# A fused attention and two mixture-of-experts layers: no score block computed twice, and the split of the turned p moved three slots ahead of its products

## The chip, the cores and the metric

One core of a Trainium2 chip runs the whole program. The metric is the device time of one execution in microseconds. TensorE (PE) does the matrix products, VectorE (DVE), ScalarE (ACT) and GpSimd (POOL) the elementwise work, SyncE (SP) issues nearly all transfers between memory and the chip's buffers.

## The reference

```
# attention without softmax: B = 8 batches, S = 3072 rows, D = 256, z has 64 columns
scores = z @ z.T / S
x = u * (max(scores, 0)**2 @ v)
# first expert layer on all 24576 rows of x: F = 1024
h = x @ w_in
solu = h * softmax(h)
ln = (solu - mean) / sqrt(var + 1e-6) * g_ln
x = ln @ w_out
# second layer: each row goes to the one of 8 experts with the largest gate
out[row] = gate * (max(x[row] @ w1[e], 0) @ w2[e])
```

## The kernel before, in words

The rows of all batches are cut into 48 chunks of 512 rows, six to a batch (below, chunk j is the chunk number j = 0 to 5 of its batch). A chunk is worked on in 24 slots, one for each block of 128 key rows. For a slot, scores come from two matmuls (`pe_scores`), ACT takes relu and square (`r`, then `a`), ACT writes the high part `ah` and DVE the low part `al` of each value (32-bit values are multiplied as sums of two parts), and PE adds six products of 512 columns to the chunk's output `o` (`pe_av`). The order of the work is written out by hand: a loop runs over slots n, and in slot n the scores of slot n + 4 (`LA` = 4) are issued, then the events that stand in a table for this slot, then `o` of slot n, then ACT's `ah` of slot n + 3 and DVE's `al` of slot n + 2. Each engine carries out its own instructions in this order.

Scores are symmetric. A block of chunk q against keys of chunk k > q is the turned block of chunk k against keys of chunk q. So the chunk that comes first stores its blocks turned (`put`: DVE transposes `a` into a buffer `sym`, one slot later SP sends it to `kept` in memory), and the later one reads them (`get`, four issues of 64 KB, 7 slots ahead of `o`: `LA` + `GA`) instead of computing. For blocks at least four chunks apart (`turn_late`) the transposing is done after the reading. One pair is left out by `again`: chunk 5 computes its four blocks against chunk 4 a second time, and chunk 4 does not store them. `order` spreads stored and computed blocks evenly over a chunk's 24 slots.

When a chunk's `o` is done, it is multiplied by u (`gate_x`, which writes `ut`) and split (`split_x`, which writes `xt`), and the first expert layer of that chunk runs as events in the 24 slots of the next one, in four blocks of 128 rows, t = 0 to 3, 6 slots apart. With w the first slot of a block: h on PE at w and w + 1, its maximum on DVE at w + 1 (line 491), the exponential on ACT and its product with h on DVE at w + 2, the 32 x 32 turning of p on DVE at w + 3 (`blk_turn`, line 512), the variance on ACT at w + 4. To finish turning, p goes through memory: `blk_put` at w + 3 writes `pb` to `moved` (line 521), `blk_get` at w + 5 reads it back as `pT` (line 527). `blk_split` makes the high half `pth` on ACT and the low half `ptl` on DVE (lines 104 and 105, in the helper `split`), in two halves at w + 9 and w + 10, and `blk_y` multiplies them with w_out at w + 10 and w + 11 (12 products each, lines 108 to 110 in the helper `mm3`). The steps that scale, route and scatter the rows follow from the slots after. The last chunk uses wider steps. After the 48th chunk the second expert layer runs over sorted rows until the end.

Of the kernel before, what the change touches and what calls it, by code (L numbers as in the profile page):

```python
# [33 lines left out]
def attention_moe_kernel(ctx, tc, u, v, z, w_in, w_out, g_ln, w_gate, w1, w2, out):  # L34
# [9 lines left out]
    NCB = S // CH  # L44
    NKB = S // P
# [4 lines left out]
    ZB = 5  # L50
# [3 lines left out]
    ZL = 8  # L54
    XA, XT0, XE = 2, 21, 23
    SA, SB, SC, SD, SH = 11, 14, 16, 19, 1
    TW, TM, X2 = 8, 2, 23
# [12 lines left out]
    SNAP = NCHUNK - 4  # L70
# [42 lines left out]
    with tc.manual_schedule():  # L113
# [4 lines left out]
                        base=-1, pattern=[[1, P]], channel_multiplier=-1)  # L118
# [13 lines left out]
    with ExitStack() as st:  # L132
# [20 lines left out]
        def at(slot, fn, *args):  # L153
            events[slot].append((fn, args))
# [3 lines left out]
        t = vp.tile([P, 2, 4, D], F32R, tag="vw", name="raw64").bitcast(I32).rearrange("p a r d -> p (a r d)")  # L158
        raw64 = [t[:, i * 2 * CH:(i + 1) * 2 * CH].rearrange("p (f two) -> p f two", two=2) for i in range(2)]
        t = mp.tile([P, F], F32, tag="pT", name="cu64").bitcast(I32)  # L160
# [159 lines left out]

        def again(q, k):
            return q == NCB - 2 and k == NCB - 1

        def turn_late(q, k):
            return q + 4 <= k

# [1 line left out]
        for par in range(min(2, B)):  # L331
            for hi in range(NCB):
                for lo in range(hi):
                    if again(lo, hi):
                        continue
                    kept[par, hi, lo] = nc.dram_tensor(f"kept_{par}_{hi}_{lo}", (4, P, CH), F32, kind="Internal").ap()
        t = [xrow.tile([P, KD * CH], F32, tag="x", name="sym") for _ in range(2)]
        t = [x[:, i * CH:(i + 1) * CH] for x in t for i in range(2)]
# [2 lines left out]

        def order(j):

            old = [kb for kb in range(4 * j) if not again(kb // 4, j)]
            new = [kb for kb in range(NKB) if kb not in old]
            return [kb for _, kb in sorted([((i + 0.5) / len(old), kb) for i, kb in enumerate(old)] +
                                           [((i + 0.5) / len(new), kb) for i, kb in enumerate(new)])]

# [7 lines left out]

        def is_kept(n):
            _, q, k, _ = block(n)
            return k < q and not again(k, q)

        def is_put(n):
            _, q, k, _ = block(n)
            return k > q and not again(q, k)

        n_put, n_get = [0], [0]
        put_t = {}
# [454 lines left out]
        for i in range(NU):  # L821
            w = HALF if i < N_CUT else units[i]
# [71 lines left out]
        for c in range(NCHUNK):  # L894
            b, j = divmod(c, NCB)
            s0 = c * NKB
            sb = b * NCB * NKB
            if b == 0:
                base = 4 * j - Z0
                zload = base - 5 + (j > 0)  # L900
                vload = 4 * j - V0
                at(base, turn_z, c)
            else:

                late = j >= NCB - 2
                base = sb + 3 + 4 * (j - NCB + 2) if late else sb - (NCB - 1 - j) * NKB + ZB
                zload = base - (4 if late else ZL)
                vload = sb - NKB + VL + VS * j
                at(base - 2, turn_z, c)
            at(zload, load_z, c)  # L910
            at(base, prep_z, c)
            if c > 0:
                at(s0 - LA - 5, swap_z, c)
            vstep = 3 if b else 2
            for h in range(2):
                at(vload + vstep * h, load_v, c, h)
                at(vload + vstep * (h + 1), prep_v, c, h)
            for x in range(4):
                at(s0 + 2 + x, load_u, c, x)
            at(s0 + 14, turn_u, c)  # L920

            last = c == NCHUNK - 1
            more = 2 if last else 1
            s1 = s0 + NKB
            for t in range(4):
                w = s1 + 2 + (TW if last else 6) * t
                at(w, blk_h, c, t, 0)
                at(w + 1, blk_h, c, t, 1)
                at(w + 1, blk_max, c, t)
                at(w + 2, blk_exp, c, t)  # L930
                at(w + 2, blk_mul, c, t)
                at(w + 3, blk_turn, c, t)
                at(w + 4, blk_var, c, t)
                at(w + 3, blk_put, c, t)
                at(w + 5, blk_get, c, t)
                y = w + 10 + TM * (t == 3 and last)
                at(y - 1, blk_split, c, t, 0)
                at(y, blk_split, c, t, 1)
                at(y, blk_y, c, t, 0)
                at(y + 1, blk_y, c, t, 1)  # L940
            e = y + 3
            for i in range(3):
                at(e + more * i, blk_scale, c, i)
            for i in range(2):
                at(e + more * (3 + i), blk_scale, c, 3)
            at(e + more * 5, blk_logits, c)
            for i in range(10):
                at(e + more * (6 + i + 2 * (i > 5)), blk_route, c, i)
            for t in range(4):
                at(e + more * (6 + 2 * t), blk_rows, c, t)  # L950
                at(e + more * (18 + 2 * t), blk_scatter, c, t)
# [7 lines left out]
        early = [(0, n_early, FULL)], False  # L959
        late = [(n_early, n_late, FULL), (n_early + n_late, n_half, HALF)], True  # L960
        for i in range(NE + 4):
            at((SNAP + 1) * NKB + 21 + 2 * i, table_step, 0, *early)
            at(after + 2 * i, table_step, 1, *late)
            at(after + 2 * i + 1, table_step, 1)
            if i < NE:
                at(after + 2 * i + 2, pad_tail, i)
# [113 lines left out]
```

## Time and profile before

| | |
|---|---|
| median of 3 runs | 4622.75 us (4619.26 to 4626.38) |
| profiled execution | 4625.15 us, its span 4623.4 us |
| busy: PE, DVE, ACT, POOL | 94%, 69%, 61%, 25% of the span |
| mean granted clock of TensorE | 0.986 of full speed |
| attention with the first expert layer | 0 to about 3393 us |
| second expert layer | from there to the end |

A busy share is an average over stages; the waits say what an engine stood idle for, and a stretch of one chunk shows what an average hides. SP has no busy share in the page: its timeline of issues shows it.

### The profile page before, as it was taken

Reading aid. Unit: us, or ns where it says so; the run is one execution under the profiler, and the core shown is the slowest. Engines: PE = TensorE matmul, PEld = TensorE weight load, DVE = VectorE, ACT = ScalarE, POOL = GpSimd, SP = SyncE. Lnnn points to the kernel's source line nnn. Section 1 sums busy time; section 2 is a strip of 40 time slices with the busy share of each in tenths; the row PEclk is TensorE's granted clock in tenths of the full one; section 3 lists DMA queues with packets and bytes.
Section 4 is the critical chain, followed back from the end, with each engine's and each line's share of the span. In section 5 each row is a group of like instructions: output and inputs, shape, how many; then the busy total and the mean of one; then the engine's idle time right before and its main releaser. Section 6 shows DMA issues by size and latency. Waiting matters only on the chain.

```text
span 4623.4 us, 74108 instructions
## 1 busy us (share of the span) xinstructions
PE 4344.6 (94%) x23458; PEld 3707.2 (80%) x23458; DVE 3195.8 (69%) x5636; ACT 2811.0 (61%) x5184; POOL 1174.6 (25%) x2346
## 2 busy tenths in 40 slices
PE   7999999999999999999999999899899999999998
PEld 5777777777777777777777777777789999999998
DVE  7677667767677766777676667767676665556676
ACT  6666665666576666656765766676454444444565
POOL 3123222322322222223222222222222211111111
PEclk8999999999999999999999999999999999999999
DMA  5687688778867886887688678767875655555575
GB/s 143 151 163 149 152 165 155 161 157 162 152 156 158 160 156 152 163 155 164 150 164 148 157 163 157 151 158 157 148 161 141 161 139 145 143 139 137 152 217 160
DMA packets 2529035, 719.21 MB, mean 156 GB/s; under 512 B 2326653, under 2 KB 2417021, under 8 KB 2528640
## 3 DMA queue, kind: packets, MB, share of 16 engines
q1 hardware_dynamic: 2509536, 663.33, 68.3%
q0 software_dynamic: 19104, 51.15, 3.3%
q8 instruction: 183, 3.00, 0.3%
q14 instruction: 212, 1.74, 0.1%
HBM read 442.46 MB, written 273.49 MB: 155 GB/s over the span
## 4 chain that ended last, share of the span: by engine, by line
PE 41%; SPq 18%; DVE 16%; DMA 15%; issue 5%; ACT 3%; POOL 0%; DVEq 0%; ACTq 0%; POOLq 0%
SPq L527 6%; SPq L391 6%; DMA sym<-kept 4%; DMA kept<-sym 4%; PE y L110 3%; PE y L108 3%; PE y L109 3%; PE g L109 3%; PE g L108 3%; PE g L110 3%; PE o L108 3%; PE o L109 3%; PE o L110 3%; PE yp L110 3%; DVE ptl L105 3%
## 5 line engine op out<-in xcount | busy, mean ns | idle before, releaser
L108 PE MATMUL o<-ah,vw 128*128 128x512 f32 x2304 | 923.3, 401 | 10.2 <-DVE ut L452 9.2
L109 PE MATMUL o<-al,vw 128*128 128x512 f32 x2304 | 915.7, 397 | 12.0 <-DVE al L428 12.0
L110 PE MATMUL o<-ah,vw 128*128 128x512 f32 x2304 | 907.4, 394 | 0.0
L413 ACT ACTIVATE r<-s 128x512 f32<-128x512 f32 x704 | 412.9, 587 | 446.4 <-PE s L408 446.3
L110 PE MATMUL yp<-gw,ptl 128*128 128x264 f32 x1536 | 471.9, 307 | 200.7 <-DVE ptl L105 199.8
L491 DVE TENSOR_REDUCE nm<-h 128x1 f32<-128x1024 f32 x192 | 234.9, 1223 | 555.7 <-PE h L479 553.4
L423 ACT ACTIVATE ah<-a 128x512 fp32r<-128x512 f32 x800 | 505.3, 632 | 134.3 <-PE o L110 39.4
L428 DVE TENSOR_TENSOR al<-a,ah 128x512 fp32r<-128x512 f32 x800 | 552.4, 693 | 10.3 <-ACT ah L423 8.8
L108 PEld LDWEIGHTS o<-ah,vw 128*128 128x128 f32 x2304 | 440.4, 191 | 103.4 <-DVE ut L452 19.2
L110 PEld LDWEIGHTS o<-ah,vw 128*128 128x128 f32 x2304 | 439.5, 191 | 97.3
L109 PEld LDWEIGHTS o<-al,vw 128*128 128x128 f32 x2304 | 440.3, 191 | 95.9 <-DVE al L428 17.6
L110 PEld LDWEIGHTS yp<-gw,ptl 128*128 128x128 f32 x1536 | 297.6, 194 | 250.9 <-DVE ptl L105 249.2
L108 PE MATMUL yp<-gw,pth 128*128 128x264 f32 x1536 | 450.6, 293 | 16.3 <-ACT pth L104 14.0
L418 ACT ACTIVATE a<-r 128x512 f32<-128x512 f32 x704 | 437.8, 622 | 26.6 <-DVE ps L632 12.9
L109 PE MATMUL yp<-gw,pth 128*128 128x264 f32 x1536 | 444.8, 290 | 0.0
L847 ACT ACTIVATE zw_x<-g 128x512 fp32r<-128x512 f32 (+1 forms) x350 | 182.6, 522 | 396.0 <-PE g L110 391.9
L848 DVE SCALAR_TENSOR_TENSOR zw_x<-g,zw_x 128x512 fp32r<-128x512 f32 (+1 forms) x350 | 208.4, 595 | 266.1 <-ACT zw_x L847 260.9
L496 ACT ACTIVATE p<-h,nm 128x1024 f32<-128x1024 f32 x192 | 214.3, 1116 | 267.5 <-DVE nm L491 267.4
L108 PEld LDWEIGHTS yp<-gw,pth 128*128 128x128 f32 x1536 | 295.9, 193 | 56.2 <-ACT pth L104 38.8
L377 DVE STREAM_TRANSPOSE sym<-a 128x512 f32<-128x512 f32 x352 | 248.6, 706 | 116.6 <-DMA kept<-sym 115.7
L508 ACT ACTIVATE p<-p,nmp 128x1024 f32<-128x1024 f32 x192 | 220.3, 1147 | 142.3 <-DVE pb L512 142.2
L644 POOL DMA_INDIRECT sorted_rows<-y,pi x192 | 200.9, 1046 | 409.8 <-DMA sorted_rows<-y,pi 346.7
(274 smaller groups left out, 10862.1 us busy)
## 6 DMA issues: line engine op xcount, KB each, us to landing
vw_x<-in_moe_w SPq DMA_DIRECT2D x124, 1024.0 KB, 5.4
sym<-kept SPq DMA_DIRECT2D x1792, 64.0 KB, 2.9
moved<-pb SPq DMA_DIRECT2D x768, 128.0 KB, 2.2
pT<-moved SPq DMA_DIRECT2D x768, 128.0 KB, 3.7
kept<-sym SPq DMA_DIRECT2D x352, 256.0 KB, 2.9
vr<-in_v SPq DMA_DIRECT2D x96, 256.0 KB, 2.9
ur<-in_u SPq DMA_DIRECT2D x384, 64.0 KB, 2.6
kept<-a SPq DMA_DIRECT2D x96, 256.0 KB, 3.4
```

The costliest lines, as they stand in the source:

```text
L108: T.matmul(out=out, lhsT=lh, rhs=rh, start=start, stop=False, **kw)
L109: T.matmul(out=out, lhsT=lh, rhs=rl, start=False, stop=False, **kw)
L110: T.matmul(out=out, lhsT=ll, rhs=rh, start=False, stop=stop, **kw)
L377: V.transpose(out=w, in_=a_t[n])
L391: nc.sync.dma_start(out=w[x * 32:(x + 1) * 32].rearrange("i (b j) -> i b j", j=32), in_=src[r, x])
L413: A.activation(out=r, in_=s_t.pop(n), func=AF.Relu)
L418: A.activation(out=a, in_=r_t.pop(n), func=AF.Square)
L423: A.activation(out=h, in_=a_t[n], func=AF.Copy)
L428: V.tensor_tensor(out=l, in0=a_t[n], in1=ah_t[n].bitcast(F32), op=ALU.subtract)
L491: V.tensor_reduce(out=s["nm"][:, t:t + 1], in_=h, axis=AX.X, op=ALU.max, negate=True)
L508: A.activation(out=p, in_=p, func=AF.Square, bias=s["nmp"][:, t:t + 1], accum_out=s["q"][:, t:t + 1])
L527: nc.sync.dma_start(out=w[y * 32:(y + 1) * 32].rearrange("j (a i) -> j a i", i=32), in_=src[y])
```

## The change

Four things change. The exception `again` goes: chunk 4 stores its four blocks against chunk 5, and chunk 5 reads them back, so that 20 of its 24 blocks are read and 4 computed. For all chunks but the last the put of p is moved from w + 3 to w + 4, the get from w + 5 to w + 8, the split from w + 9 and w + 10 to w + 12 and w + 13, the products from w + 10 and w + 11 to w + 15 and w + 16; scaling, routing and scattering follow the products and so move by 5 slots. The loads of z of the last two chunks of the next batch, which came late because the old rows were needed longer, now come by the rule of the others. A step that makes the table of experts moves by 5 slots.

```diff
--- before.py
+++ after.py
@@ -320,10 +320,6 @@
 
 
 
-
-        def again(q, k):
-            return q == NCB - 2 and k == NCB - 1
-
         def turn_late(q, k):
             return q + 4 <= k
 
@@ -331,8 +327,6 @@
         for par in range(min(2, B)):
             for hi in range(NCB):
                 for lo in range(hi):
-                    if again(lo, hi):
-                        continue
                     kept[par, hi, lo] = nc.dram_tensor(f"kept_{par}_{hi}_{lo}", (4, P, CH), F32, kind="Internal").ap()
         t = [xrow.tile([P, KD * CH], F32, tag="x", name="sym") for _ in range(2)]
         t = [x[:, i * CH:(i + 1) * CH] for x in t for i in range(2)]
@@ -341,8 +335,8 @@
 
         def order(j):
 
-            old = [kb for kb in range(4 * j) if not again(kb // 4, j)]
-            new = [kb for kb in range(NKB) if kb not in old]
+            old = list(range(4 * j))
+            new = list(range(4 * j, NKB))
             return [kb for _, kb in sorted([((i + 0.5) / len(old), kb) for i, kb in enumerate(old)] +
                                            [((i + 0.5) / len(new), kb) for i, kb in enumerate(new)])]
 
@@ -356,11 +350,11 @@
 
         def is_kept(n):
             _, q, k, _ = block(n)
-            return k < q and not again(k, q)
+            return k < q
 
         def is_put(n):
             _, q, k, _ = block(n)
-            return k > q and not again(q, k)
+            return k > q
 
         n_put, n_get = [0], [0]
         put_t = {}
@@ -901,10 +895,8 @@
                 vload = 4 * j - V0
                 at(base, turn_z, c)
             else:
-
-                late = j >= NCB - 2
-                base = sb + 3 + 4 * (j - NCB + 2) if late else sb - (NCB - 1 - j) * NKB + ZB
-                zload = base - (4 if late else ZL)
+                base = sb - (NCB - 1 - j) * NKB + ZB
+                zload = base - ZL
                 vload = sb - NKB + VL + VS * j
                 at(base - 2, turn_z, c)
             at(zload, load_z, c)
@@ -931,11 +923,13 @@
                 at(w + 2, blk_mul, c, t)
                 at(w + 3, blk_turn, c, t)
                 at(w + 4, blk_var, c, t)
-                at(w + 3, blk_put, c, t)
-                at(w + 5, blk_get, c, t)
-                y = w + 10 + TM * (t == 3 and last)
-                at(y - 1, blk_split, c, t, 0)
-                at(y, blk_split, c, t, 1)
+
+                out_, back, cut_, y = (3, 5, 9 + TM * (t == 3), 10 + TM * (t == 3)) if last else (4, 8, 12, 15)
+                at(w + out_, blk_put, c, t)
+                at(w + back, blk_get, c, t)
+                cut_, y = w + cut_, w + y
+                at(cut_, blk_split, c, t, 0)
+                at(cut_ + 1, blk_split, c, t, 1)
                 at(y, blk_y, c, t, 0)
                 at(y + 1, blk_y, c, t, 1)
             e = y + 3
@@ -959,7 +953,7 @@
         early = [(0, n_early, FULL)], False
         late = [(n_early, n_late, FULL), (n_early + n_late, n_half, HALF)], True
         for i in range(NE + 4):
-            at((SNAP + 1) * NKB + 21 + 2 * i, table_step, 0, *early)
+            at((SNAP + 1) * NKB + 26 + 2 * i, table_step, 0, *early)
             at(after + 2 * i, table_step, 1, *late)
             at(after + 2 * i + 1, table_step, 1)
             if i < NE:
```

On DVE, the last block of chunk 2 shows where the split stands before the sum of its products. In the kernel before, L105 writes `ptl` from `pT`, L428 is `al`, L512 turns p, and L550 takes the finished product `yp`:

```order
L105 TENSOR_TENSOR ptl_3296<-pT,pth_3295 128x512
L512 STREAM_TRANSPOSE pb<-p 128x1024
L285 TENSOR_TENSOR zw<-zt,zw 64x512
L428 TENSOR_TENSOR al<-a,ah 128x512
L105 TENSOR_TENSOR ptl_3328<-pT,pth_3327 128x512
L428 TENSOR_TENSOR al<-sym,ah 128x512
L550 SCALAR_TENSOR_TENSOR y<-gw_sum,nmp,yp 128x264
```

In the changed kernel (line numbers lower by 6: L422 is `al`, L485 the maximum, L495 and L497 the product with h, L506 the turning, L371 a `put`, L544 takes `yp`) the same block reads:

```order
L105 TENSOR_TENSOR ptl_3350<-pT,pth_3349 128x512
L422 TENSOR_TENSOR al<-a,ah 128x512
L105 TENSOR_TENSOR ptl_3378<-pT,pth_3377 128x512
L485 TENSOR_REDUCE nm<-h 128x1
L422 TENSOR_TENSOR al<-sym_151,ah 128x512
L495 SCALAR_TENSOR_TENSOR p,spm<-h,p 128x1024
L497 TENSOR_SCALAR nmp<-spm 128x1
L422 TENSOR_TENSOR al<-sym_152,ah 128x512
L506 STREAM_TRANSPOSE pb<-p 128x1024
L422 TENSOR_TENSOR al<-a,ah 128x512
L371 STREAM_TRANSPOSE sym<-a 128x512
L544 SCALAR_TENSOR_TENSOR y<-gw_sum,nmp,yp 128x264
```

Between the second half's split and the taking of `yp` stand now three `al` and the maximum, product and turning of another block, where one `al` stood before.

On SP, the middle of chunk 4 of the second batch. Before (L391 a get from `kept`, L521 a put of p, L527 a get of p, `x4` four issues):

```order
L521 DMA moved_1<-pb_8159 32x1024 x4
L391 DMA sym1_152<-kept_1_4_3 32x16x32 x4
L527 DMA pT_8241<-moved_1 32x32x32 x4
L391 DMA sym2_153<-kept_1_4_3 32x16x32 x4
L391 DMA sym3_154<-kept_1_4_3 32x16x32 x4
L391 DMA sym_150<-kept_1_4_3 32x16x32 x4
L521 DMA moved_2<-pb_8345 32x1024 x4
L391 DMA sym_150<-kept_1_5_0 32x16x32 x4
L527 DMA pT_8418<-moved_2 32x32x32 x4
L391 DMA sym0_151<-kept_1_5_0 32x16x32 x4
```

And after (L385 a get, L515 a put of p, L521 now the get of p, L377 a store of chunk 4's blocks, L268 a load of z):

```order
L515 DMA moved_1<-pb_8121 32x1024 x4
L377 DMA kept_1_5_4<-sym_149 128x512
L385 DMA sym0_151<-kept_1_4_3 32x16x32 x4
L385 DMA sym1_152<-kept_1_4_3 32x16x32 x4
L377 DMA kept_1_5_4<-sym_149 128x512
L521 DMA pT_8263<-moved_1 32x32x32 x4
L385 DMA sym2_153<-kept_1_4_3 32x16x32 x4
L385 DMA sym3_154<-kept_1_5_0 32x16x32 x4
L515 DMA moved_2<-pb_8309 32x1024 x4
L377 DMA kept_1_5_4<-sym_149 128x512
L385 DMA sym_150<-kept_1_5_0 32x16x32 x8
L268 DMA zd_8429<-in_z 32x16x32 x4
```

Stores and a load of z stand in a stretch that had none, and the get of p (`pT`) follows its put (`moved`) at a greater distance.

## Rows read from the trace of the kernel before

**Rows 1.** Profile page, part 1: busy time, share of the span, instructions.

```profile
PE 4344.6 (94%) x23458; PEld 3707.2 (80%) x23458; DVE 3195.8 (69%) x5636; ACT 2811.0 (61%) x5184; POOL 1174.6 (25%) x2346
```

**Rows 2.** PE's waits, whole span: who waited for whom, us, times, longest.

```profile
PE yp L110 <- DVE ptl L105: 199.8, 217, 4.7
PE yp L108 <- ACT pth L104: 14.0, 19, 1.5
PE o L109 <- DVE al L428: 12.0, 10, 2.8
PE o L108 <- DVE ut L452: 9.2, 34, 1.0
```

**Rows 3.** Waits of all engines, whole span, same columns.

```profile
PEld yp L110 <- DVE ptl L105: 249.2, 228, 4.9
ACT ah L423 <- DMA sym<-kept: 40.8, 41, 1.9
```

**Rows 4.** Timeline, one block: start, length in us, engine, line, operation, idle before.

```profile
1501.91 0.28 PE L108 MATMUL yp<-gw,pth 128*128 128x264 f32 x1
1502.03 0.28 PE L109 MATMUL yp<-gw,pth 128*128 128x264 f32 x1
1502.20 0.69 DVE L105 TENSOR_TENSOR ptl<-pT,pth 128x512 fp32r<-128x512 f32 x1
1502.94 0.39 PE L110 MATMUL yp<-gw,ptl 128*128 128x264 f32 x1 [0.63 <-DVE ptl L105]
```

**Rows 5.** Stretches of chunks 0, 1 and 4 of the third batch.

```profile
core 0: us, PE busy (x) PEld busy (x) DVE busy (x) ACT busy (x) POOL busy (x), PEclk, DMA share, GB/s
861.90:940.50 78.60, 70.97 (x337) 59.20 (x336) 56.52 (x96) 55.52 (x100) 22.54 (x48) 0.95 0.70 168
940.50:1011.50 71.00, 67.27 (x330) 55.94 (x329) 49.59 (x87) 51.43 (x93) 17.10 (x42) 0.99 0.70 156
...
1147.50:1213.90 66.40, 62.07 (x307) 50.80 (x306) 45.22 (x78) 38.27 (x69) 18.52 (x42) 1.00 0.86 147
```

**Rows 6.** Timeline of SP, chunk 4 of that batch, first and last rows.

```profile
1147.59 1.82 SPq L521 DMA_DIRECT2D moved<-pb  x4
...
1203.26 6.63 SPq L391 DMA_DIRECT2D sym<-kept  x12
1212.80 2.23 SPq L521 DMA_DIRECT2D moved<-pb  x4
```

**Rows 7.** PE's waits behind 3393 us.

```profile
PE yp L110 <- DVE ptl L105: 1.8, 4, 1.2
```

**Rows 8.** SP's own waits, whole span, the longest in total.

```profile
SPq L521 <- DVE pb L512: 420.5, 135, 7.6
```

**Rows 9.** Timeline of PE, a score pair's first and the matmul behind it.

```profile
1508.43 0.39 PE L407 MATMUL s<-zw 128*128 128x512 f32 x1
1508.88 0.40 PE L475 MATMUL h<-w_in,xt 128*128 128x512 f32 x1
```

**Rows 10.** Costliest groups by line: count, busy us, mean ns of one.

```profile
L413 ACT ACTIVATE r<-s 128x512 f32<-128x512 f32 x704 | 412.9, 587 | 446.4 <-PE s L408 446.3
L377 DVE STREAM_TRANSPOSE sym<-a 128x512 f32<-128x512 f32 x352 | 248.6, 706 | 116.6 <-DMA kept<-sym 115.7
```

**Rows 11.** Timeline, one store of a kept block.

```profile
1499.91 0.43 SPq L383 DMA_DIRECT2D kept<-sym  x1
```

**Rows 12.** Transfers in chunk 4: packets, main queue, one kind of issue.

```profile
DMA packets 56524, 9.75 MB, mean 148 GB/s; under 512 B 55852, under 2 KB 55852, under 8 KB 56518
q1 hardware_dynamic: 56326, 9.13, 83.7%
sym<-kept SPq DMA_DIRECT2D x64, 64.0 KB, 3.1
```

**Rows 13.** PE's waits in chunks 0 to 2, then 3 to 5.

```profile
PE yp L110 <- DVE ptl L105: 13.9, 13, 4.1
...
PE yp L110 <- DVE ptl L105: 10.7, 14, 1.3
```

## The prediction

> **What bounds the kernel now.** I first read how busy each engine is: TensorE (PE) works 94% of the span, VectorE (DVE) 69%, ScalarE (ACT) 61% [rows 1]. So PE is the bound, and the question is what makes up its idle time. The table of PE's waits answers: 199.8 us in 217 waits of the product `yp` for `ptl`, and then nothing above 14 us [rows 2]. `ptl` is the low half of the turned p, made by `blk_split` (line 105 on DVE, after its high half `pth` on ACT). The same wait, seen at the weight loads, is 249.2 us in 228 waits [rows 3]. One such wait is in the timeline [rows 4]: PE issues the first two products of a block at 1501.91 and 1502.03, DVE begins `ptl` at 1502.20 and PE goes on at 1502.94. PE simply reached the products before DVE had come to the split, which stands only one slot earlier in its own stream.
>
> The second thing to see is the stage table [rows 5]: chunk 0 of a batch lasts 78.6 us at a clock of 0.95, chunk 1 71.0 us at 0.99, chunk 4 66.4 us at 1.00; chunks 2, 3 and 5 are much like chunk 4. The third is SyncE (SP), which issues nearly all transfers. In chunk 4 its timeline [rows 6] shows issues back to back: 21 rows from 1147.59 to 1209.89 hold 60.1 us of issuing; then come 2.9 us without one. There SP is as full as PE.
>
> **The split stands three slots ahead.** PE's product `o` of slot n needs `al` of slot n, which DVE gets in slot n - 2. So PE cannot be more than two slots further in the program than DVE. The split now stands in slots w + 12 and w + 13, its products in w + 15 and w + 16. Before PE starts `yp` it has done `o` of the slot ahead, whose `al` DVE issued after that split. The wait for `ptl` should therefore go altogether, in all chunks but the last one, which keeps its numbers. From 199.8 us I take 1.8 us that fall behind 3393 us, where the last chunk's blocks run [rows 2, 7]: 198.0 us in 213 waits. A wait costs more than the idle time shown. In [rows 4] PE starts 0.91 us after the product before, where a running pair is 0.12 us apart (1501.91 to 1502.03): 0.79 us lost, 0.63 shown. With 0.16 us for each of 213 waits the gain is 198.0 + 34 = **232 us**. Bounds: 198.0, and the 249.2 us of the weight loads. The wait for `pth` goes with it: 14.0 us in 19 waits [rows 2], 17 with the refills; a part belongs to the last chunk, so I take **15 us** (bounds 10 and 17).
>
> What could be late next? DVE has to deliver `al` and ACT `ah` at PE's new pace. DVE is busy 45 to 57 us and ACT 38 to 56 us of a chunk, and chunks would last 61 to 73 us [rows 5], and PE waits for `al` today only 12.0 us in 10 waits [rows 2]. The split's two DVE steps (0.69 us each, [rows 4]) now come just ahead of the maximum of the block after next, where before they came behind the turning of p. In those slots PE has two h groups and two yp groups to do, so there is room. I let the present waits for `al` and for `ut` double: 12.0 + 9.2 = **21 us lost** [rows 2].
>
> Put of p one slot later, get four slots behind it: SP now waits 420.5 us for DVE's turned p [rows 8]. That wait should nearly go, which lets SP run ahead; on PE's path this is worth nothing by itself. The route steps move by 5 slots with their products; POOL, which does them, is busy 17 to 23 us of a chunk [rows 5].
>
> **All scores kept.** In each of 8 batches 4 blocks of chunk 5 are now read back instead of computed. PE loses 32 pairs of matmuls. In [rows 9] the matmul behind a pair starts 0.45 us after the pair's first: **14 us gained**. ACT loses 32 relus of 587 ns and their squares, DVE gets 32 transposes of 706 ns [rows 10], in chunk 4, where it is busy 45 of 66 us [rows 5]; neither is on the path. The price is SP's: 4 puts and 16 get issues a batch. By the order of SP's issues, the stretch from one chunk's first `ur` load to the next one's holds in chunk 4 now 120 issues instead of 104 (8 gets, 4 puts, 4 loads of z that came later before), in chunk 5 99 instead of 91, in chunk 0 77 instead of 81. A get costs SP 6.63 / 12 = 0.55 us, a put 0.43 us [rows 6, 11], the z issue is taken as a get: 8 x 0.55 + 4 x 0.43 + 4 x 0.55 = 8.3 us. SP's 62.3 us of chunk 4 become 70.6 us. PE without its waits would need about 61 us there (66.4 less 4.3 idle and the refills). So SP falls behind by some 9.6 us in each chunk 4, and regains it in chunks 5 and 0.
>
> How much of that reaches PE? Gets stand 7 slots ahead (`GA` + `LA`), 7 x 66.4 / 24 = 19 us; four issues (2.2 us), landing (3.1 us [rows 12]), and `ah` and `al`, taken as 0.69 us each like the split's step of the same shape [rows 4], need 6.7 us. On paper 12 us are spare, and then nothing is lost. But ACT waited for `sym` from memory in 41 places (40.8 us, [rows 3]), so part of this is in use. Between 0 and 12 us of cover I choose 5, since those waits are short: 4.6 us lost a batch, **37 us** in eight (bounds 0 and 77).
>
> The DMA engines have the same trouble. In chunk 4 the 56326 packets of SP's queue take 83.7% of 16 engines over 66 us [rows 12], 55.2 us, or 0.98 ns a packet; a get of 64 KB in runs of 128 bytes is 512 packets, 0.5 us, so 16 more issues need about 8 us: 64 us against PE's 61. The Trainium skill (page DMA: Bandwidth & Descriptors, section Why small descriptors are slow (HBM only)) says that each small packet carries a fixed cost besides its bytes. By that rule, which speaks against fetching in short runs what PE computes in 0.45 us, the engines would be a limit of chunk 4 as well, and the sum would be the third case's below; that nearly all packets here are under 512 B (55852 of 56524, [rows 12]) agrees with its premise.
>
> **The sum.** The profiled execution took 4625.15 us (span 4623.4), 2.4 us above the median of the three runs. 4625 - 232 - 15 - 14 + 21 + 37 = 4422 us, less 2.4 gives 4420 in terms of the median. In chunk 0 of a batch the clock is 0.95 and in chunk 1 0.99 [rows 5]: 3.9 + 0.7 us a batch, 37 us in eight, that PE would have at full clock. I take a quarter of it, 10 us, as regained, since fewer waits precede those stretches: **4410 us**.
>
> **Rivals.**
> Faster still (0.20): SP's lateness stays under its cover, and the clock stays at its upper level through chunks 0 and 1. Then 37 us of loss fall away and 27 more are regained: 4410 - 64 = 4346, about 4345 us. For it speaks that chunk 0, with 7.6 us of PE idle, is the one with low clock, while chunk 4, with 4.3 us idle, is at 1.00 [rows 5]. Against it: chunk 0 also has 24 fresh scores and the heaviest DVE and ACT load. The Trainium skill (page TensorE: Matmul & The Clock Gate, section HAM oscillation — how this bites in real kernels) holds that waits between groups of matmuls bring the array back to half rate; by that rule this case is the likelier one, and [rows 5] agree in direction.
>
> SP sets the pace from chunk 3 on (0.18): the gain is then that of chunks 0 to 2 alone, 13.9 of 24.6 us of the wait [rows 13], that is 0.565 x 247 = 140 us; chunk 4 gets longer by 70.6 - 66.4 = 4.2 us, 34 us in eight; the scores bring nothing. 4623 - 140 + 34 = 4517 us. For it: [rows 6]. Against it: SP still waits for DVE elsewhere [rows 8], and most waits for `ptl` are the short ones of the program's order, not late data.
>
> No change (0.03): the wait moves whole to `al`, because DVE paces the chunk: 4620 us. Against: DVE's busy time, 45 to 57 us of a chunk [rows 5].
>
> Slower (0.04): SP's issue is what paces every chunk. Then the 160 issues more (5310 against 5150) at 0.55 us come on top: 4623 + 88 = 4711 us. It decides from the point at which SP has no idle time left in chunks 0 to 2. Against: its waits of 420.5 us for p [rows 8].
>
> **How the numbers follow.** The forecast has 0.55. Its own range is 4375 to 4460 (SP's cover 0 or 12 us, `yp` between its bounds). The range for 8 in 10 reaches over the faster case to 4320 and up to 4520 for the one in which SP sets the pace. About 0.2% (9 us) is what a measurement here can tell from no change: faster 0.55 + 0.20 + 0.18 = 0.93, same 0.03, slower 0.04.
>
> **What would show it.** Right: no wait of `yp` for `ptl` over 10 us in total; 672 instead of 704 score matmuls of each kind; chunks 1 to 3 shorter by 4 to 6 us each; chunk 4 shorter by 1 to 4 us; SP's wait for the turned p far below 420 us; ACT's wait for `sym` larger, in chunks 4 and 5. Wrong: a new large wait of `o` for `al` or of `yp` for `pth`; chunk 4 as long as now or longer; chunk 0 no shorter.

## The result and the profile after

The changed kernel takes 4496.11 us (median of 4 runs, 4486.59 to 4498.83), the kernel before on the same chip 4621.36 us (4 runs): a ratio of 0.9724, with a 95% interval of 0.9707 to 0.9741. It is faster by 125 us, where 4410 us had been forecast. The profiled execution is the fastest of the four: 4486.59 us, its span 4484.9.

From the page of the changed kernel, busy time in part 1 and two groups of part 5:

```profile
PE 4274.7 (95%) x23394; PEld 3678.7 (82%) x23394; DVE 3235.9 (72%) x5668; ACT 2781.2 (62%) x5120; POOL 1123.5 (25%) x2346
...
L407 ACT ACTIVATE r<-s 128x512 f32<-128x512 f32 x672 | 393.5, 586 | 134.3 <-PE s L402 134.0
...
L417 ACT ACTIVATE ah<-sym 128x512 fp32r<-128x512 f32 x384 | 240.7, 627 | 176.1 <-DMA sym<-kept 156.0
```

There are 672 computed blocks in place of 704, as the change says. PE's busy time fell by 69.9 us [rows 1], its idle time by 68.6 (from 4623.4 - 4344.6 = 278.8 to 4484.9 - 4274.7 = 210.2). The 32 pairs of matmuls that went are 14 us of the busy time [rows 9]. The rest is not less work: counted from one product's start to the next one's, those of `yp`, as many as before, took 78 us less, and those of `o` 22 us more. PE's waits in the changed kernel:

```profile
PE o L109 <- DVE al L422: 131.6, 91, 5.8
PE o L108 <- DVE ut L446: 21.0, 16, 2.9
PE g L108 <- DVE zw_x L842: 14.2, 3, 7.5
...
PE yp L110 <- DVE ptl L105: 4.1, 2, 3.6
```

The wait for `ptl`, 199.8 us before [rows 2], is 4.1 us; the one for `pth` is gone. In their place `o` waits 131.6 us for `al`, where it had waited 12.0 [rows 2]; the prediction had named such a wait as a sign of being wrong. SyncE's own waits show the same shift. Its put of the turned p waits 36.2 us instead of 420.5 [rows 8]; the load of v (L299), which matters further down, waits 118.6 us for DVE to be done with the buffer:

```profile
SPq L299 <- DVE vw L311: 118.6, 50, 5.3
...
SPq L515 <- DVE pb L506: 36.2, 46, 2.3
```

The stretches of the third batch, chunk 0 to chunk 5 (columns: from:to, length, busy PE, PEld, DVE, ACT, POOL, granted clock, DMA share, GB/s):

```profile
825.20:897.50 72.30, 68.46 (x337) 55.97 (x336) 53.91 (x93) 53.81 (x99) 21.23 (x48) 1.00 0.73 181
897.50:961.20 63.70, 63.70 (x322) 53.90 (x322) 49.88 (x86) 51.47 (x93) 15.24 (x42) 1.00 0.78 175
961.20:1024.50 63.30, 63.30 (x326) 53.82 (x325) 50.37 (x87) 45.85 (x83) 16.48 (x42) 1.00 0.83 174
1024.50:1086.60 62.10, 62.10 (x319) 52.82 (x319) 49.87 (x85) 42.02 (x76) 17.60 (x42) 1.00 0.91 177
1086.60:1152.00 65.40, 60.25 (x306) 50.32 (x305) 48.36 (x84) 38.01 (x68) 18.24 (x42) 1.00 0.84 160
1152.00:1226.70 74.70, 65.73 (x309) 53.87 (x307) 49.20 (x84) 38.10 (x68) 21.42 (x48) 0.93 0.86 155
```

In chunks 1 to 3 PE has no idle time at all: the length of the stretch is its busy time. Chunk 0 went from 78.6 to 72.3 us, chunk 1 from 71.0 to 63.7, chunk 4 from 66.4 to 65.4 [rows 5]. Chunk 5 went the other way, to 74.7 us at a clock of 0.93. In the kernel before it reads:

```profile
1213.90:1280.60 66.70, 62.97 (x313) 51.95 (x313) 47.60 (x84) 40.58 (x73) 22.05 (x48) 1.00 0.78 151
```

The gain is in chunks 0 to 3, and a little in chunk 4; chunk 5 gives a part of it back.

SyncE's timeline in the first half of that chunk 5 (start, duration, line, transfer):

```profile
1161.02 4.20 SPq L385 DMA_DIRECT2D sym<-kept  x8
1165.27 2.08 SPq L318 DMA_DIRECT2D ur<-in_u  x4
1167.39 2.20 SPq L385 DMA_DIRECT2D sym<-kept  x4
1169.70 3.18 SPq L521 DMA_DIRECT2D pT<-moved  x4
1172.93 1.19 SPq L318 DMA_DIRECT2D ur<-in_u  x2
```

Each row ends about 0.1 us or less before the next one begins. SyncE has no gap in chunk 4 either (its pauses over 0.3 us come to 0.4 us there, as a mean over the batches 2 to 8), and so it enters chunk 5 late. How this reaches PE is seen in the timeline of all engines a little later:

```profile
1181.55 0.40 SPq L299 DMA_DIRECT2D vr<-in_v  x1
1181.90 0.40 PE L108 MATMUL o<-ah,vw 128*128 128x512 f32 x1
...
1185.54 0.61 POOL L310 TENSOR_SCALAR vw<-vr 128x512 fp32r<-128x512 f32 x1 [11.76 <-DMA vr<-in_v]
1186.19 0.69 DVE L311 TENSOR_TENSOR vw<-vr,vw 128x512 fp32r<-128x512 f32 x1 [3.93 <-POOL vw L310]
1186.80 0.68 DVE L422 TENSOR_TENSOR al<-sym,ah 128x512 fp32r<-128x512 f32 x1
1187.53 0.80 PE L109 MATMUL o<-al,vw 128*128 128x512 f32 x1 [5.24 <-DVE al L422]
1188.13 0.63 PE L110 MATMUL o<-ah,vw 128*128 128x512 f32 x1
```

PE stands 5.24 us for `al`, but `al` is not what is late. Read backwards, DVE stood 3.93 us at its share of v (`vw`, line 311), because GpSimd had waited 11.76 us for v from memory, which SyncE had issued at 1181.55, when its full list came to it. DVE carries out its instructions in order, so the `al` behind has to wait. A row of PE's waits names the last link; the first one is two engines further back. What this one link is worth is tested below, with v issued by GpSimd.

### The profile page after: what moved, and what is told of

It reads as the page before. It is cut to its first block, busy times and chain, and to the rows that moved or that the text cites. A ratio compares the mean times of both kernels' runs of the same rounds, so it can differ in the third digit from the quotient of the medians.

```text
span 4484.9 us, 74503 instructions
## 1 busy us (share of the span) xinstructions
PE 4274.7 (95%) x23394; PEld 3678.7 (82%) x23394; DVE 3235.9 (72%) x5668; ACT 2781.2 (62%) x5120; POOL 1123.5 (25%) x2346
## 4 chain that ended last, share of the span: by engine, by line
PE 56%; SPq 13%; DMA 12%; DVE 10%; issue 5%; ACT 3%; POOL 1%; DVEq 0%; POOLq 0%; ACTq 0%
PE o L108 6%; PE o L109 6%; PE o L110 6%; SPq L385 6%; SPq L521 3%; PE y L110 3%; PE y L108 3%; PE y L109 3%; PE g L108 3%; PE g L109 3%; PE g L110 3%; DMA sym<-kept 3%; PE h L469 2%; PE h L473 2%; PE h L470 2%
## 5 line engine op out<-in xcount | busy, mean ns | idle before, releaser
L109 PE MATMUL o<-al,vw 128*128 128x512 f32 x2304 | 929.1, 403 | 131.9 <-DVE al L422 131.6
L422 DVE TENSOR_TENSOR al<-a,ah 128x512 fp32r<-128x512 f32 x768 | 529.5, 690 | 30.2 <-ACT ah L417 26.5
L417 ACT ACTIVATE ah<-a 128x512 fp32r<-128x512 f32 x768 | 485.4, 632 | 104.6 <-DVE a L391 76.1
L105 DVE TENSOR_TENSOR ptl<-pT,pth 128x512 fp32r<-128x512 f32 x384 | 269.1, 701 | 321.6 <-ACT pth L104 316.8
L407 ACT ACTIVATE r<-s 128x512 f32<-128x512 f32 x672 | 393.5, 586 | 134.3 <-PE s L402 134.0
L110 PE MATMUL yp<-gw,ptl 128*128 128x264 f32 x1536 | 442.4, 288 | 4.2 <-DVE ptl L105 4.1
L412 ACT ACTIVATE a<-r 128x512 f32<-128x512 f32 x672 | 417.5, 621 | 37.5 <-DMA kept<-a 19.6
L417 ACT ACTIVATE ah<-sym 128x512 fp32r<-128x512 f32 x384 | 240.7, 627 | 176.1 <-DMA sym<-kept 156.0
L371 DVE STREAM_TRANSPOSE sym<-a 128x512 f32<-128x512 f32 x384 | 270.4, 704 | 78.7 <-DMA kept<-sym 78.4
L485 DVE TENSOR_REDUCE nm<-h 128x1 f32<-128x1024 f32 x192 | 234.5, 1221 | 124.9 <-PE h L473 124.8
L638 POOL DMA_INDIRECT sorted_rows<-y,pi x192 | 216.7, 1129 | 370.6 <-DMA sorted_rows<-y,pi 308.6
```

Source lines behind the costliest of these rows:

```text
L105: V.tensor_tensor(out=lo, in0=src, in1=hi.bitcast(F32), op=ALU.subtract)
L109: T.matmul(out=out, lhsT=lh, rhs=rl, start=False, stop=False, **kw)
L110: T.matmul(out=out, lhsT=ll, rhs=rh, start=False, stop=stop, **kw)
L371: V.transpose(out=w, in_=a_t[n])
L407: A.activation(out=r, in_=s_t.pop(n), func=AF.Relu)
L412: A.activation(out=a, in_=r_t.pop(n), func=AF.Square)
```

## The experiments

Ratios are to the kernel before on the same chip. "Chunk 4 takes 61.1 us" and the like are means over the batches 2 to 8, from the end of one chunk's `gate_x` to that of the next; SyncE's issue time is the sum of its issues in the same stretch.

**The split alone.** The kernel before with only the new slots of put, get, split and products (and of the table step). Chunk 5 still computes its four blocks.

```diff
-                at(w + 3, blk_put, c, t)
-                at(w + 5, blk_get, c, t)
-                y = w + 10 + TM * (t == 3 and last)
+                out_, back, cut_, y = (3, 5, 9 + TM * (t == 3), 10 + TM * (t == 3)) if last else (4, 8, 12, 15)
+                at(w + out_, blk_put, c, t)
+                at(w + back, blk_get, c, t)
```

> The kernel before with the split alone moved (put, get, split, products and what follows), the four blocks of chunk 5 still computed twice. Theory A, the kept scores load SP's queue in chunks 4 and 5 and cost more there than they save: chunk 5 falls from 74 to 62-64 us, chunk 4 to 62-64 us, and the kernel takes 4380 to 4420 us, clearly less than the changed kernel's 4496. Theory B, the late slots of p's own put and get make chunk 5 longer, the kept scores are innocent: chunk 5 stays near 74 us and the kernel takes 4500 to 4520 us (the scores' 14 us come back).

Measured: 4416.66 us, ratio 0.9573 (0.9557 to 0.9589). The whole change is at 0.9724, so the other part costs 0.0151 of about 4616 us (the kernel before, on the two chips), 70 us. Chunks 1 to 3 are those of the changed kernel (63.9, 63.3, 62.1 us). Chunk 0 takes 2.8 us more than in the changed kernel, and chunk 5 took 66.5 us, more than the 62 to 64 expected. What keeping all scores costs is in the last two chunks, for which the stretches of its third batch read, chunk 4 and chunk 5:

```profile
1070.40:1131.10 60.70, 60.08 (x308) 50.72 (x307) 45.73 (x79) 38.61 (x69) 17.66 (x42) 1.00 0.90 155
1131.10:1197.40 66.30, 62.76 (x304) 52.55 (x303) 48.58 (x84) 40.59 (x74) 22.18 (x48) 0.95 0.86 154
```

Against the changed kernel's 65.4 and 74.7 us, keeping all scores costs 4.7 and 8.4 us in this batch, although PE has four pairs of matmuls less to do in chunk 5.

**All scores kept, alone.** The changed kernel with the old slots.

```diff
-                out_, back, cut_, y = (3, 5, 9 + TM * (t == 3), 10 + TM * (t == 3)) if last else (4, 8, 12, 15)
+                at(w + 3, blk_put, c, t)
+                at(w + 5, blk_get, c, t)
+                y = w + 10 + TM * (t == 3 and last)
```

> The kernel before with all scores kept alone, split and products where they were. Theory A: slower than before, by 4 to 10 us a batch, 4650 to 4700 us, with chunks 4 and 5 longer than 66.5 us. Theory B: about 4605 us, before less the 14 us of scores.

Measured: 4679.36 us, ratio 1.0145 (1.0128 to 1.0162): slower by 67 us. The two parts are thus independent within what is measured: 0.9573 x 1.0145 = 0.9712 beside 0.9724. PE's waits in this kernel:

```profile
PE yp L110 <- DVE ptl L105: 185.0, 214, 3.1
PE yp L108 <- ACT pth L104: 65.1, 45, 6.9
PE o L109 <- DVE al L422: 22.8, 20, 3.4
```

The wait for `ptl` is back, which is the split's own. The one for `pth` rose from 14.0 [rows 2] to 65.1 us: with SyncE late, the get of p is late.

**Half of the kept blocks.** Split moved; chunk 4 stores all four blocks, chunk 5 reads two and computes two, and the late loads of z stay late.

```diff
+        def again(q, k, r):
+            return q == NCB - 2 and k == NCB - 1 and r >= 2
```

> The split moved, chunk 4 stores all four blocks, chunk 5 reads two of its four blocks against chunk 4 and computes the other two; z of the last two chunks loaded late as before. Theory A: chunk 5 between that of the split alone and 74 us, about 67 to 70, and the kernel at 4430 to 4465 us. Theory B: no different from the changed kernel within 10 us, 4490 to 4510.

Measured: 4440.71 us, ratio 0.9635 (0.9619 to 0.9651). Chunk 4 takes 63.1 us and chunk 5 69.5, between the 61.1 and 66.5 of the split alone and the 64.7 and 74.4 of the whole change. The loss grows with the number of blocks read, but the second step, from half to all, also brings the loads of z forward; no run parts the two.

**The put of p from ACT's queue.** In chunks 4 and 5 only, so that SyncE has fewer issues.

```diff
-                nc.sync.dma_start(out=moved[t][:, x], in_=w[x * 32:(x + 1) * 32])
+                q_ = nc.scalar if c % NCB in (NCB - 3, NCB - 2) else nc.sync
+                q_.dma_start(out=moved[t][:, x], in_=w[x * 32:(x + 1) * 32])
```

> The changed kernel with p's put issued from ScalarE's queue in the blocks that run in chunks 4 and 5 (16 issues of 64 of a chunk's loads less on SP, same bytes, same packets). If SP's issuing is the limit (theory A1), chunk 5 gets 5 to 8 us shorter and the kernel takes 4420 to 4460 us. If the 16 DMA engines are the limit (theory A2), chunk 5 stays at 72 to 75 us and the kernel within 15 us of 4496.

Measured: 4543.62 us, ratio 0.985 (0.9833 to 0.9866), slower than the changed kernel, which no theory had said. SyncE's issue time did fall, from 58.6 to 49.6 us in chunk 4 and from 62.9 to 55.1 in chunk 5, yet the chunks took 69.8 and 77.3 us. ACT's wait for `pT` rose from 110.3 to 202.2 us: the put now comes in ACT's own order, and the get of p on SyncE's list stands behind the put's landing (SyncE waits 119.0 us for it), with the gets of `sym` behind it. SyncE's pauses rose from 0.4 to 14.2 us in chunk 4 and from 5.4 to 17.9 in chunk 5. This run made a new wait and by itself settles nothing about issues against DMA engines. The next two do.

**More issues, the same bytes and packets.** The put of p in 8 issues instead of 4, in chunks 4 and 5.

```diff
-                nc.sync.dma_start(out=moved[t][:, x], in_=w[x * 32:(x + 1) * 32])
+                n = 2 if c % NCB in (NCB - 3, NCB - 2) else 1
+                for i in range(n):
+                    js = slice(i * 32 // n, (i + 1) * 32 // n)
+                    nc.sync.dma_start(out=moved[t][js, x], in_=w[x * 32 + js.start:x * 32 + js.stop])
```

> The changed kernel with each put of p in the blocks that run in chunks 4 and 5 cut into 8 issues of 16 rows instead of 4 of 32: 16 more issues on SP in each of these chunks, about 0.4 us each, the same bytes in the same packets. If SP's issuing is the limit (A1), chunks 4 and 5 get 6 us longer each, some 50 to 100 us in all: 1.011 to 1.022 times the changed kernel, ratio to before 0.983 to 0.994. If the DMA engines are the limit (A2), no change: ratio 0.970 to 0.976.

Measured: 4574.97 us, ratio 0.9924 (0.9908 to 0.9941). The 32 issues more of a batch make SyncE's issue time longer by 4.1 us in chunk 4 and 6.5 in chunk 5, and the chunks get longer by 4.6 and 6.6 us. The stretches of its third batch, chunks 4 and 5:

```profile
1111.20:1180.90 69.70, 61.79 (x306) 51.48 (x305) 48.67 (x84) 38.01 (x69) 17.47 (x42) 0.98 0.85 150
1180.90:1260.80 79.90, 66.54 (x307) 54.65 (x307) 49.63 (x84) 38.25 (x68) 21.47 (x48) 0.91 0.87 144
```

The DMA share, 0.85 and 0.87, is that of the changed kernel (0.84 and 0.86), over longer stretches. The packets on SyncE's queue in the third batch's chunks 4 and 5 are nearly as many as in the changed kernel, 116170 against 115899. Only issues were added, and they cost their own time.

**Half of the bytes of the gets.** In chunks 4 and 5 each get of `sym` reads half of its columns.

```diff
-                nc.sync.dma_start(out=w[x * 32:(x + 1) * 32].rearrange("i (b j) -> i b j", j=32), in_=src[r, x])
+                n = 8 if q >= NCB - 2 else 16
+                nc.sync.dma_start(out=w[x * 32:(x + 1) * 32].rearrange("i (b j) -> i b j", j=32)[:, :n], in_=src[r, x][:, :n])
```

> The changed kernel with each get of chunks 4 and 5 reading only half of its columns: as many issues on SP, half the packets and bytes of these gets (the other half of the buffer keeps old values, so the output is not the reference's). If the DMA engines are the limit (A2), chunk 5 falls from 74 to 62-64 us and chunk 4 to 62 us: ratio to before 0.945 to 0.955. If SP's issuing is the limit (A1), only what an issue gets shorter comes back (from 0.53 to perhaps 0.45 us, 5 us a chunk at most): ratio 0.958 to 0.970, and SP's timeline in chunk 5 still without gaps.

Measured: 4422.58 us, ratio 0.9595 (0.9579 to 0.9611). In its third batch:

```profile
1073.80:1134.80 61.00, 59.66 (x306) 50.39 (x305) 48.62 (x84) 37.76 (x68) 17.26 (x42) 1.00 0.69 135
1134.80:1204.00 69.20, 62.60 (x300) 51.52 (x300) 49.82 (x84) 37.89 (x67) 21.29 (x48) 0.95 0.70 136
```

The DMA share fell to 0.69 and 0.70, and the chunks by 3.7 and 3.8 us. SyncE's issue time fell by the same 3.7 us in each, since a get of half as many pieces of 128 bytes is issued sooner (median 453 ns instead of 487). By itself the run would fit a limit of the DMA engines as well; with the one before, in which no byte was added, the issue time is what both have in common. Nor does an issue get longer when the DMA engines are fuller: in the changed kernel the median of a get is 487 ns in each of the chunks 1 to 5, at DMA shares from 0.78 to 0.91.

**u issued by GpSimd.** In chunks 4 and 5 the eight loads of u leave SyncE's list; in the changed kernel, and in the kernel with the split alone.

```diff
-                nc.sync.dma_start(out=u_raw[c][x * 32:(x + 1) * 32, k].rearrange("i (a j) -> i a j", j=32), in_=src[k, x])
+                (nc.gpsimd if c % NCB >= NCB - 2 else nc.sync).dma_start(out=u_raw[c][x * 32:(x + 1) * 32, k].rearrange("i (a j) -> i a j", j=32), in_=src[k, x])
```

In the changed kernel:

> The changed kernel with the loads of u of chunks 4 and 5 issued by GpSimd: 8 issues less on SP in each of these chunks, the same bytes, and a queue on which nobody waits closely for u. A1: 4 us less of issuing in each, chunk 4 back to 62 us and chunk 5 5 to 8 us shorter: ratio 0.955 to 0.962. A2: unchanged, ratio 0.970 to 0.976.

With the split alone:

> The split moved, chunk 5's four blocks computed twice as before, and the loads of u of chunks 4 and 5 issued by GpSimd. The split alone was at 0.9573 of before. If SP's issuing still holds up chunk 5 there (A1): 0.950 to 0.954, chunk 5 at 62 us. If not: 0.956 to 0.959.

Measured: 4456.83 us, ratio 0.9671 (0.9655 to 0.9687), in the changed kernel, with chunk 5 at 71.4 us instead of 74.4; and 4391.78 us, ratio 0.953 (0.9513 to 0.9546), with the split alone, chunk 5 at 63.8 us instead of 66.5. Transfers of the same bytes from another engine's list help. In the changed kernel the ratio lies between the two forecasts and in neither, since chunk 4 got no more than 0.8 us shorter. The DMA share rose, to 0.96 and 0.91 in chunks 4 and 5 of the third batch there and to 0.95 and 0.92 with the split alone, and the chunks got shorter all the same.

**v issued by GpSimd.** The changed kernel, with the loads of v of the next batch off SyncE's list. They fall into chunk 5 and the chunk 0 behind it.

```diff
-            nc.sync.dma_start(out=t, in_=rows(v, c).rearrange("(h r p) d -> h p r d", h=2, p=P)[h])
+            (nc.gpsimd if c >= NCB else nc.sync).dma_start(out=t, in_=rows(v, c).rearrange("(h r p) d -> h p r d", h=2, p=P)[h])
```

> The changed kernel, but v of the next batch (from the second batch on, two loads of 256 KB for each of six chunks, which fall in chunk 5 and the chunk 0 behind it) is issued by GpSimd, which also prepares it, and no longer by SyncE. In the changed kernel DVE stands at its share of v (vw) for 72.2 us in all behind GpSimd, which waits for the load 219.4 us; of PE's waits for al in the chunks 5 of all batches some 25 us fall into such a stand of DVE. Theory A (one late transfer on SyncE's list makes DVE stand, and al behind it): SyncE's list of chunk 5 loses about six issues and their waits, chunk 5 gets 3 to 6 us shorter, 4450 to 4470, ratio 0.965 to 0.970, PE's wait for al falls from 131.6 to about 100 us. Rival (only the number of gets on SyncE's list counts; or GpSimd, which waits for other things in its own order, issues v later than SyncE did): chunk 5 as long as before or longer, ratio 0.972 or above.

Measured: 4430.95 us, ratio 0.9607 (0.9588 to 0.9625), better than either theory said, and in another place than theory A had it. Chunk 5 takes 73.4 us instead of 74.4. Chunk 0 takes 65.7 instead of 72.7, and PE has no idle time left in it; chunk 1 gets 1.1 us longer, and the stage after the last chunk is 8.6 us shorter. In the third batch:

```profile
819.70:885.10 65.40, 65.40 (x330) 55.31 (x329) 53.94 (x94) 54.30 (x99) 26.39 (x55) 1.00 0.78 194
```

Why chunk 0: v has one buffer, and the next load of v waits on SyncE's list until DVE has worked the last one up. SyncE's waits in the changed kernel's chunk 0 (825 to 897 us), then all engines' in the same stretch:

```profile
SPq L299 <- DVE vw L311: 14.7, 6, 4.3
```

```profile
DVE sym L371 <- DMA kept<-sym: 10.2, 5, 2.8
```

While SyncE stands 14.7 us at v, the puts of `sym` stand behind it; DVE stands 10.2 us for a free `sym`, and PE 2.9 us for `al`. With v on GpSimd's list DVE stands there 1.8 us, and GpSimd waits for the buffer of v in SyncE's place.

For chunk 5 this run corrects the reading above. PE's wait for `al` fell to 101.3 us, as theory A said, but in the chunks 5 only from 74.9 to 65.1. Of these, DVE's standing at v went from 25 to 0.3 us, and its standing at the split of p rose from 6 to 10. The late v was a true link of that chain and not the bound: with it gone, DVE stands longer for the next late transfer, and most of the wait for `al` is left. In this kernel's chunk 5 the DMA share is 1.01, so that there the DMA engines may be a limit too; no run tests that.

**The time after the last chunk.** From the end of the last chunk's `gate_x` to the end of the program the kernel before takes 1230.1 us, the changed one 1254.0, the split alone 1255.2. The changed kernel's timeline there, GpSimd, DVE and PE:

```profile
3246.03 1.07 POOL L638 DMA_INDIRECT sorted_rows<-y,pi  x1 [0.97 <-DMA pT<-moved]
3256.72 0.97 POOL L883 DMA_INDIRECT out_y<-a_x,ids  x1 [9.62 <-ACT a_x L882]
...
3271.83 0.97 POOL L638 DMA_INDIRECT sorted_rows<-y,pi  x1 [8.81 <-DMA gi<-sorted_rows]
3276.75 0.97 POOL L638 DMA_INDIRECT sorted_rows<-y,pi  x1 [3.96 <-DMA sorted_rows<-y,pi]
...
3279.39 0.49 DVE L544 SCALAR_TENSOR_TENSOR y<-gw_sum,nmp,yp 128x264 f32<-128x264 f32 x1 [8.81 <-issue]
...
3281.73 0.58 PE L108 MATMUL g<-vw_x,zd_x 128*128 128x256 f32 x1 [7.45 <-DVE zw_x L842]
```

The scatters of a chunk's rows (L638, one for each of its four blocks), five slots later than before, now stand among the first stores of the second layer (L883) on GpSimd. DVE stands at the last chunk's `y`, whose buffer is still to be scattered, and PE at `g` behind DVE. Three kernels test that, all on the base of the split alone with u on GpSimd (ratio 0.953, of which this stage takes 1249.4 us). The four scatters of a chunk in one slot, for two chunks:

```diff
-                at(e + more * (18 + 2 * t), blk_scatter, c, t)
+                at(e + more * (18 + (0 if NCHUNK - 4 < c < NCHUNK - 1 else 2) * t), blk_scatter, c, t)
```

> The kernel is the one with the split moved, chunk 5 computing its pairs against chunk 4, and u of chunks 4 and 5 issued by GpSimd; in it the four scatters of sorted rows of the chunks 45 and 46 (counted from 0) all stand in one slot, so that on GpSimd they come ahead of the first two stores of the second layer instead of three behind them. That kernel took 0.953 of the time before, and after its last attention chunk PE waited 8.0 and 5.4 us at two places where DVE stood still: once at y of the last chunk, whose buffer is still to be scattered by GpSimd (8.4 us), once at yi, behind vv of GpSimd, which stands behind the same scatters (6.2 us). Theory A (the scatters' place, five slots later than in the kernel before, is the late loss): both stalls go, 10 to 14 us less, 4378 to 4382, ratio 0.950 to 0.951, and the two waits of DVE are under 2 us. Rival (the second layer's own loads and weights are late there, whatever GpSimd does): 4390, ratio 0.953, the stalls of PE stay or move by no more than 3 us.

A third buffer for `y`:

```diff
-            y_t[c] = mp.tile([P, 4, RW], F32, tag="y", name="y", bufs=2)
+            y_t[c] = mp.tile([P, 4, RW], F32, tag="y", name="y", bufs=3)
```

> The same kernel as a base, scatters where they were, but a third buffer for y, so that the last chunk's y need not wait for the scatter of the chunk two ahead. Theory A (DVE held up by the buffer of y): the first stall of PE (8.0 us) goes, the second (5.4 us, GpSimd's order) stays: 4383 to 4386, ratio 0.951 to 0.952. Rival (the loads of the second layer set the time): 4390, ratio 0.953.

Both:

> Both edits together on the same base. Theory A: no more than the scatters' place alone, 4376 to 4382, ratio 0.949 to 0.951. Rival (the loads of the second layer set the time): 4390, ratio 0.953.

Measured: 4378.21 us, ratio 0.9498 (0.9484 to 0.9512), for the scatters; 4387.17, 0.9514 (0.9501 to 0.9527), for the buffer; 4381.54, 0.9501 (0.9488 to 0.9514), for both. GpSimd with the scatters in one slot (L644 and L889 are the scatter and the store in this kernel):

```profile
3165.66 0.97 POOL L644 DMA_INDIRECT sorted_rows<-y,pi  x1 [5.27 <-DMA sorted_rows<-y,pi]
3168.38 0.97 POOL L644 DMA_INDIRECT sorted_rows<-y,pi  x1 [1.74 <-DMA sorted_rows<-y,pi]
3171.07 1.26 POOL L644 DMA_INDIRECT sorted_rows<-y,pi  x1 [1.72 <-DMA sorted_rows<-y,pi]
3172.63 0.97 POOL L889 DMA_INDIRECT out_y<-a_x,ids  x1 [0.31 <-issue]
```

Both stands of DVE are gone, and PE's waits at `g` for `zw_x` with them; the stage takes 1233.4 us. The times of the three kernels overlap in part, and those of the buffer with the base's, so the buffer's smaller gain rests on the trace: it takes away the stand at `y`, but not the one behind `vv`. Of the 19.3 us that this stage took above the kernel before, the scatters' place accounts for 16 (12 in the kernel with both edits, where the stage takes 1237.4). The kernel with the scatters first is the fastest that was run, 0.977 of the changed kernel (0.9498 / 0.9724).

## Why the prediction was right, and where its sizes were off

The direction, the mechanism of the first part and the range for 8 in 10 held; the forecast's own range, 4375 to 4460 us, did not, and the forecast was 86 us too low. Three terms make this up: the stage after the last chunk (24), the cost of all scores (70 instead of 23) and the split (some 222 instead of 236). The profiled executions differ by 138.5 us (4623.4 to 4484.9) and the medians by 125, since the profiled execution of the changed kernel was the fastest of its four and that of the kernel before was 4 us above its median.

**The split: right, its size in part by luck.** Waits of `yp` for `ptl` came to 4.1 us, and `pth` is gone. The forecast for this part, with its losses at `al` and `ut` and the 10 us of clock, was -232 - 15 + 21 - 10 = -236 us. With the split alone the span up to the end of the last chunk fell from 3393.3 to 3158.8 us, by 234.5, but between two chips: on that of the split alone the kernel before took 4611 us and not 4621. By its ratio it gains 0.0427 of 4611, 197 us, or 222 without the 25 lost behind the last chunk. Its parts shifted, and errors cancelled: the losses at `al` were larger (83.2 us in that kernel, where 24 were forecast for the whole change), the gain in chunk 1 too: 8.5, 5.4 and 5.0 us in chunks 1 to 3 instead of 4 to 6 each. The step that failed here is that `al` had room at PE's new pace. The wait comes with the split: 83.2 us for `al` with the split alone, 22.8 with all scores kept alone, 131.6 with both. Whether the new pace brings it or the new place of the split's own steps on DVE, no run parts.

**The 5 slots of routing and scattering: put at nothing, wrongly.** The text costed them by POOL's busy time, 17 to 23 us of a chunk, and left out what they collide with behind the last chunk. It is a loss of 24 us, of which the scatters' place is 12 to 16 on the base where it was tested. The busy share was the wrong view; what mattered was which instructions of the same engine stand around the moved ones.

**All scores kept: the term that was mis-sized.** Forecast: 37 us lost by SyncE's lateness, 14 gained by PE, 23 net, and a larger wait of ACT for `sym` as its mark. The mark came, 156.0 us instead of 40.8 [rows 3], but the price was another. Measured: 70 us net (0.0151 of the time), or 67 on the kernel before. Two steps of the term failed. First, "regains it in chunks 5 and 0": in chunk 4 the loss is 3.6 us a batch, near the 4.6 of the text, but chunk 5 loses 7.9 more and only chunk 0 gains (2.8). SyncE's issue time there is 62.9 us against 54.7 with the split alone. The late issues of chunk 4 and the 16 own gets together leave nothing to regain. Second, the cover of 5 us was taken from the gets' distance alone. A late list delays everything on it, v and the get of p too, and DVE stands at each of these with `al` behind it. Of the 131.6 us for `al`, summed by chunk, 74.9 fall into chunks 5, 18.5 into chunks 4 and 38.2 into chunks 0 (15.7 of these into the very first chunk). In 36 of the 131.6 DVE itself stood, 25 of these at v; in the rest DVE was at work, and that this was on what had piled up is argued, not shown.

**The rivals.** "SP sets the pace from chunk 3 on", 4517 us, was nearest to the measured 4496, by luck in part. Its place was wrong: chunk 3 has no idle time on PE and gained 5.0 us, and the bound begins in chunk 4. It had chunk 4 longer by 4.2 us, where it got shorter by 1.8, and nothing for chunk 5 and the stage behind the last chunk, where the losses are. That the DMA engines are the limit, the other ground the text gave for it, is not borne out. Chunk 3 runs at full pace with a DMA share of 0.91, above chunk 4's 0.84, and 32 issues more a batch with no byte more cost 11.2 us. The rule of the Trainium skill (page DMA: Bandwidth & Descriptors, section Why small descriptors are slow (HBM only)) on the fixed cost of a small packet is therefore not what sets the time of chunks 4 and 5 here.

**The clock.** Chunk 0 came to 1.00 as hoped, but chunk 5 fell from 1.00 to 0.93, and the mean is 0.986 in both kernels. Added up, the time at the lower of the two clock levels fell from 78 to 3 us in the chunks 0 and 1 of batches 2 to 8, more than the quarter that was forecast; it rose from 11 to 65 us in their chunks 4 and 5 and from 12 to 36 behind the last chunk. So the term was right where it was put, and other waits gave its gain away. With the split alone the mean is 0.990. Chunk 0's length was put down to the clock too readily. With the clock at 1.00 it still took 72.7 us, and 65.7 when v left SyncE's list.

What stays open: why the stage after the last chunk keeps some 3 us more than before with the scatters first (1233.4 against 1230.1; in the kernels that leave the scatters where they are it varies by more, from 1245.3 to 1255.6), how much the earlier loads of z cost, and how much of chunk 5's loss is left if the scatters, u and v are all moved, which was not run.

## What to carry to other kernels

An engine that only issues transfers can be the bound of a stage. Add up its issue times in that stage, late issues of the stage before included, before giving it more; here 10.6 us of added issues a batch cost 11.2 us. When a wait names an instruction that is short and early in its engine's order, look at what that engine stood at just before it, and follow that back to the first transfer that was late. Then test it: v, found so in chunk 5, was worth 1.0 us there and 7.0 in chunk 0. When a step is moved by some slots, look at the last time it runs, where its neighbours are others.

## What was not expected of the hardware

An issue's own time on SyncE depends on the shape it describes: a get of `sym` took a median of 487 ns, and 453 ns with half the columns; four gets of p took 3.18 us in the rows above, 0.80 us each. And the granted clock fell with a single wait: the 5.24 us for `al` in chunk 5 are followed by products of 0.63 us a piece where they had taken 0.40. The stretch behind it, in the changed kernel's table of stretches:

```profile
1187.40:1192.70 5.30, 5.17 (x18) 4.68 (x19) 3.80 (x7) 3.46 (x7) 0.47 (x2) 0.50 0.65 135
```

The granted clock is 0.50, the lower of its two levels (1.2 GHz), with PE busy 5.17 of 5.30 us: the wait is paid a second time by the work behind it. The Trainium skill (page TensorE: Matmul & The Clock Gate, section HAM oscillation — how this bites in real kernels) says that waits between groups of matmuls bring the array back to half rate, and these rows agree in direction.
